# One order for all five engines, made by a planner inside the kernel: linear attention and two matrix products with sub-product tricks, on one core

## The chip, the core and the metric

The kernel runs on one core of a Trainium2 chip. Five engines take part: PE (matmul), DVE and POOL (elementwise work), ACT (elementwise work and functions) and SP, which here does nothing but start DMA transfers. Each engine runs its own instructions strictly in the order in which the program lists them; an instruction whose data or buffer is not ready holds everything behind it on that engine. The metric is the time of one execution on the device, in microseconds.

## The reference, cut to what matters

```
q, k, v: 8 batches x 8 heads x 576 x 64, float32;  the weights are float64
q_s = softmax(q, axis=-1);  k_s = softmax(k, axis=2)        # over d; over the sequence
kv  = einsum('bhsd,bhse->bhde', k_s, v)
x   = einsum('bhsd,bhde->bhse', q_s, kv)  -> 4608 tokens x 512
x   = max(x @ w_in, 0)**2 @ w_out                           # w_in 512 x 2048
out = (silu(x @ w_gate) * (x @ w_val)) @ w_out2             # w_gate, w_val 512 x 1536
```

## The kernel before

The 4608 tokens are cut into nine blocks of 512. Every product keeps float32 accuracy by splitting each operand into a rounded part and a rest ("hi" on ACT, `split`; "lo" by a subtraction, mostly on DVE) and multiplying three times (`mm3`, line 119). So PE's work is a long row of 128x512 matmuls, and each new operand costs an ACT and a DVE instruction before it.

There are four stretches. In the first, block 0 goes through attention and the first network; the order of all five engines is written out there as a list of step names (`FIRST_BLOCK`, line 381), and the change leaves this list alone. In the second, which I call the block stretch, blocks 1 to 4 go through the first network plainly: for each of 16 slices of the hidden layer 12 matmuls into a tile `ph`, then relu, square and split to a tile `g`, then 12 matmuls into `acc`. Beside it run the attention of the later blocks (`kv_unit`, `q_unit`: one for each block and pair of heads, results kept in DRAM as `x1d`) and the preparation of weights. In the third, the pair stretch, blocks 5 to 8 go through the first network as two pairs, with seven products in place of eight (`first_in`, `first_out`), in two halves each. In the fourth all blocks go through the second network the same way (`gated`, `out_stage`).

The seven products need sums of quarters of the weights, split into hi and lo. This preparation is one long generator, `work`: for the first network it loads float32 words that block 0 left in DRAM (`first_operands`); for the second it loads float64 weights (tile `wraw`), makes float32 words of them with one ACT and three DVE instructions (`bits_of`, tile `wbits`), forms four sums of quarters on POOL into new tiles `wsum` (lines 280 and 339), splits them into a staging tile `wst` (`stage`, line 252; there is one such tile until the last pair) and stores that in `hd`, `ad`, `gvd` or `od`. The stores are started from ACT's queue. A slice of a weight matrix pair is one set: 16 sets for the first network and 18 for the second. `Stream` later brings the operands back, 512 KB at a time, into five slots `wu`; a load waits until PE has left its slot.

What sets the order: SP's and PE's instructions run in the order of the program text (`manual_schedule`), where a counter (`Clock`, `attend`, `first_tick`) calls a step of attention or preparation at fixed places between matmul groups. The order of DVE, ACT and POOL is made by the framework's own scheduler.

Of the kernel before, what the change touches and what calls it, by code (L numbers as in the profile page):

```python
# [8 lines left out]
F32 = mybir.dt.float32  # L9
# [13 lines left out]
def tile_linear_attention_two_mlps(  # L23
# [12 lines left out]

# [45 lines left out]
    raws = st_prep.enter_context(tc.tile_pool(name="raws", bufs=2, side="right"))  # L96
    cv = st_prep.enter_context(tc.tile_pool(name="cv", bufs=5, side="right"))
# [39 lines left out]
    def bits_of(raws_):  # L137

        todo = []
        for raw in raws_:
            low, high = (
                raw.bitcast(I32).rearrange("p (n t) -> p n t", t=2)[:, :, t] for t in (0, 1)
            )
            w = cv.tile([P, T], I32, name="wbits", tag="wbits")
            todo.append((low, high, w, w))
        for low, high, w, t in todo:
            nc.scalar.activation(f32(t), f32(high), AF.Copy, scale=2.0**-112)  # L150
        for low, high, w, t in todo:
            nc.vector.tensor_scalar(
                t, t, 3, 0x7FFFFFFF, op0=ALU.logical_shift_left, op1=ALU.bitwise_and
            )
        for low, high, w, t in todo:
            nc.vector.scalar_tensor_tensor(
                t, low, 29, t, op0=ALU.logical_shift_right, op1=ALU.bitwise_or
            )
        for low, high, w, t in todo:
            nc.vector.scalar_tensor_tensor(  # L160
                w, high, -2**31, t, op0=ALU.bitwise_and, op1=ALU.bitwise_or
            )
        return [f32(w) for low, high, w, t in todo]

    class Weights:

        def __init__(self, src, order, borrow):
            self.src, self.order, self.borrow = src, order, borrow  # L170
            self.n_load = 0
            self.raw, self.done = {}, {}

        def load(self):
# [6 lines left out]
            if self.n_load <= 2 * self.borrow:  # L181
                t = w_slot(self.n_load - 1).rearrange("p t n -> p (t n)").bitcast(w.dtype)
            else:
                t = raws.tile([P, T], w.dtype, name="wraw", tag="wraw")
# [3 lines left out]
        def steps(self, n, pool):  # L188
# [18 lines left out]
            w = cv.tile([P, T], I32, name="wbits", tag="wbits")  # L207
# [15 lines left out]
    def w_slot(n):  # L223
# [7 lines left out]
        NF,  # L231
    )


    late = []

    def store(to, src, ticks=0):
        if ticks:
            late.append((clock.now + ticks, to, src))
        else:  # L240
            nc.sync.dma_start(to, src)

    def flush(until=None):
        for x in list(late):
            if until is None or x[0] <= until:
                nc.sync.dma_start(x[1], x[2])
                late.remove(x)

    stages = [(stp, "wst")]
    staged = [0]  # L250

    def stage():
        pool, tag = stages[staged[0] % len(stages)]
        staged[0] += 1
        return pool.tile([P, 2, 2, U], F32R, name="wst", tag=tag)

    made = set()

    def operands(kind, f):

        w, by_rows = {"gate": (w_gate, False), "val": (w_val, False), "out": (w_out2, True)}[kind]
        raw = []
        for s in (f, NG + f):
            t = raws.tile([P, T], w.dtype, name="wraw", tag="wraw")
            raw_load(w, by_rows, s, t)
            raw.append(t)
        yield
        first, = bits_of(raw[:1])
        yield
        second, = bits_of(raw[1:])  # L270
        yield
        a, b = first[:, 0:U], first[:, U:2 * U]
        c, d = second[:, 0:U], second[:, U:2 * U]

        def sums(n):
# [1101 lines left out]
```

## Time and profile before

| | |
|---|---|
| three runs | 1795.64, 1797.52 and 1800.48 us; median 1797.52 |
| the profiled execution | 1802.7 us, of which the span of its instructions is 1800.9 us |
| granted TensorE clock, mean over the span | 0.973 of full speed |
| block 1 to the last pair | from 123.5 to 1015.4 us, 891.9 us |

The two ends of the last row are the first matmul of block 1's attention product and the first matmul of the second network, read from the order of time on PE. The three terms of the kernel's time that matter below are PE's busy time in a stretch, its idle time there, and the clock that the chip granted; a clock of 1.00 is 2.4 GHz, and 0.50 would be the lower level of 1.2 GHz.

### The profile page before, as it was taken

How to read it: one execution, taken by the hardware profiler on the slowest of the kernel's cores; microseconds unless marked ns; L12 is line 12 of the kernel's file. 1: busy time of each engine (PE TensorE's matmuls, PEld its weight loads, DVE VectorE, ACT ScalarE, POOL GpSimd, SP SyncE). 2: the span in 40 equal slices, each digit the busy share in tenths (PEclk: the TensorE clock that was granted, in tenths of full speed). 3: DMA queues.
4: the chain of work that ended last, by engine and by line, in shares of the span. 5: the costliest groups of instructions: out<-in, count | busy, mean ns of one | idle time of the engine just before them, and what ended most of it. 6: DMA issues, size and time to landing. Idle time of an engine off the chain costs nothing.

```text
span 1800.9 us, 23969 instructions
## 1 busy us (share of the span) xinstructions
PE 1685.1 (94%) x8210; PEld 1366.9 (76%) x8210; DVE 1113.8 (62%) x1775; ACT 867.4 (48%) x1520; POOL 470.1 (26%) x428
## 2 busy tenths in 40 slices
PE   7999889989899898989898899999999999999998
PEld 5786667767677676867676678888888888888898
DVE  8874354565565476586868684854684568436656
ACT  7764344455455455454545453633463345334434
POOL 4753323331222422162313142101110220111011
PEclk9999999999999998999999899999999999999999
DMA  9958867655555496778788797786768667766897
GB/s 303 283 159 259 280 201 218 190 185 167 178 173 186 163 261 206 230 242 308 234 314 290 243 301 218 267 250 193 219 216 241 191 220 227 228 193 205 233 389 267
DMA packets 275017, 419.99 MB, mean 233 GB/s; under 512 B 126288, under 2 KB 167248, under 8 KB 274896
## 3 DMA queue, kind: packets, MB, share of 16 engines
q1 hardware_dynamic: 246992, 368.51, 65.9%
q10 hardware_dynamic: 27904, 49.95, 7.6%
q8 instruction: 66, 1.08, 0.2%
q14 instruction: 55, 0.45, 0.1%
HBM read 317.19 MB, written 101.19 MB: 232 GB/s over the span
## 4 chain that ended last, share of the span: by engine, by line
PE 57%; DMA 15%; DVE 9%; ACT 5%; POOL 4%; issue 3%; SPq 2%; ACTq 1%; DVEq 0%; POOLq 0%
PE ps L122 52%; DMA gvd<-wst 3%; DMA hd<-wst 3%; PE ph L122 2%; PE acc L122 2%; DVE wst L117 2%; DVE uo L117 2%; ACT wst L116 1%; DMA ad<-wst 1%; DMA wraw<-in_moe_w_val_dram 1%; DVE w L117 1%; DMA wraw<-in_moe_w_gate_dram 1%; DMA e<-x1d 1%; POOL wsum L280 1%; POOL wsum L339 1%
## 5 line engine op out<-in xcount | busy, mean ns | idle before, releaser
L122 PE MATMUL ps<-w,wu 128*128 128x512 f32 (+1 forms) x3192 | 682.6, 375 | 11.5 <-ACT ps L785 4.8
L122 PEld LDWEIGHTS ps<-w,wu 128*128 128x128 f32 x3192 | 567.7, 190 | 122.0 <-ACT ps L785 5.6
L122 PE MATMUL ps<-uo,wu 128*128 128x512 f32 (+1 forms) x1932 | 436.1, 386 | 24.0 <-DVE uo L117 21.7
L122 PEld LDWEIGHTS ps<-uo,wu 128*128 128x128 f32 x1932 | 351.5, 193 | 102.8 <-DVE uo L117 29.5
L122 PE MATMUL acc<-g,w 128*128 128x512 f32 x960 | 257.9, 416 | 22.0 <-ACT g L116 15.7
L117 DVE TENSOR_TENSOR uo<-u,uo 128x512 fp32r<-128x512 f32 (+1 forms) x322 | 229.8, 731 | 68.1 <-ACT uo L116 67.4
L116 ACT CAST uo<-u 128x512 fp32r<-128x512 f32 (+1 forms) x322 | 186.9, 592 | 159.4 <-PE ps L122 82.9
L122 PE MATMUL ph<-xT,w 128*128 128x512 f32 x960 | 247.7, 405 | 5.5 <-ACT xT L116 3.4
L122 PEld LDWEIGHTS acc<-g,w 128*128 128x128 f32 x960 | 185.7, 198 | 72.4 <-ACT g L116 18.9
L122 PEld LDWEIGHTS ph<-xT,w 128*128 128x128 f32 x960 | 180.0, 192 | 50.4 <-ACT xT L116 4.6
L953 POOL TENSOR_TENSOR u<-u 128x512 f32<-128x512 f32 (+1 forms) x30 | 35.4, 1180 | 619.2 <-DVE u L949 619.2
L948 DVE TENSOR_TENSOR u<-u,ps 128x512 f32<-128x512 f32 (+1 forms) x60 | 38.1, 634 | 195.1 <-ACT u L947 195.1
L900 ACT COPY ps<-ps 128x512 f32<-128x512 f32 x126 | 72.3, 574 | 136.1 <-PE ps L122 131.4
L117 DVE TENSOR_TENSOR wst<-wsum,wst 128x512 fp32r<-128x512 f32 x68 | 57.7, 848 | 117.3 <-ACT wst L116 117.3
L540 POOL TENSOR_TENSOR qs<-qs,qm 128x512 f32<-128x512 f32 x28 | 36.0, 1285 | 229.6 <-DVE qm L539 211.1
L116 ACT CAST wst<-wsum 128x512 fp32r<-128x512 f32 x68 | 48.2, 710 | 99.0 <-DMA gvd<-wst 27.3
L280 POOL TENSOR_TENSOR wsum<-wbits 128x256 f32<-128x256 f32 x36 | 35.2, 992 | 188.3 <-DVE wbits L160 112.8
L117 DVE TENSOR_TENSOR w<-x,w 128x512 fp32r<-128x512 f32 (+1 forms) x78 | 60.6, 785 | 23.6 <-ACT w L116 23.5
L117 DVE TENSOR_TENSOR g<-r,g 128x512 fp32r<-128x512 f32 x64 | 50.4, 788 | 39.0 <-ACT g L116 38.8
L605 ACT ACTIVATE r<-ph 128x512 f32<-128x512 f32 x64 | 38.2, 597 | 66.7 <-PE ph L122 41.1
L116 ACT CAST w<-x 128x512 fp32r<-128x512 f32 (+1 forms) x84 | 48.1, 585 | 43.6 <-PE ps L122 8.0
L339 POOL TENSOR_TENSOR wsum<-wsum 128x256 f32<-128x256 f32 x64 | 52.0, 812 | 52.0 <-DMA wsum<-w1d_out 21.3
(192 smaller groups left out, 1784.5 us busy)
## 6 DMA issues: line engine op xcount, KB each, us to landing
wu<-gvd SPq DMA_DIRECT2D x210, 512.0 KB, 4.4
wu<-od SPq DMA_DIRECT2D x105, 512.0 KB, 4.3
wu<-hd SPq DMA_DIRECT2D x56, 512.0 KB, 5.3
wu<-ad SPq DMA_DIRECT2D x56, 512.0 KB, 4.7
gvd<-wst ACTq DMA_DIRECT2D x84, 256.0 KB, 3.3
od<-wst ACTq DMA_DIRECT2D x42, 256.0 KB, 4.4
w<-in_moe_w_in_dram SPq DMA_DIRECT2D x16, 512.0 KB, 7.1
w<-in_moe_w_out_dram SPq DMA_DIRECT2D x16, 512.0 KB, 7.1
```

The lines of the kernel that those rows point to most:

```text
L116: nc.scalar.copy(hi, src)
L117: (eng or nc.vector).tensor_tensor(lo, src, f32(hi), op=ALU.subtract)
L122: nc.tensor.matmul(ps, lhsT=w[s], rhs=x[t], start=start and n == 0, stop=stop and n == 2, skip_group_check=more,)
L280: nc.gpsimd.tensor_tensor(to, x, y, op=op)
L339: nc.gpsimd.tensor_tensor(to, x, y, op=op)
L540: nc.gpsimd.tensor_tensor(t, t, m.unsqueeze(3).to_broadcast([P, TJ, 2, D]), op=ALU.add)
L605: nc.scalar.activation(r, ph, AF.Relu)
L900: nc.scalar.copy(x, y)
L948: nc.vector.tensor_tensor(u, u, gate, op=ALU.mult)
L953: nc.gpsimd.tensor_tensor(s1, a21, a22, op=ALU.add)
```

## The change

From block 1 to the end of the last pair all five engines now run in an order that a class `Plan` makes while the kernel is built. Each piece of work is a generator of steps. A step names its engine, a duration in microseconds, what it needs, which buffers it takes and frees, and, for a DMA, how long the data takes to land. `run` takes the step that can start first, and among those of its engine that could start within 0.3 us of it the one of the lowest rank (PE's chain through the blocks has helpers of rank 0, attention 2, weight preparation 5). Durations are constants in the code: 0.6 us for a 128x512 ACT instruction, 0.68 to 0.7 for one of DVE, 4.0 to 5.0 for a landing.

Along with it:

- `wst` has three buffers in place of one (two lent by the raw loads while the first network's sets are prepared), and its stores are started from SP, no longer from ACT, until the pairs are done.
- The four sums of quarters are made in place, on DVE, where POOL made them in new tiles.
- In `q_unit` POOL's subtraction of the maximum and ACT's exponential over 128x512 become eight ACT instructions of 128x64 that add the maximum as a bias and give the row sums; a DVE reduction goes.
- In the pairs the square after the relu moves from one DVE instruction to two of ACT, and the remaining POOL additions (`u`, `st`, `x`) move to DVE.
- More of the second network's sets are prepared later: counted in the two programs, raw loads in the block stretch, the pair stretch and after it go from 18, 14 and 4 to 9, 18 and 9. All later blocks' keys and values and most queries are handled in the block stretch (24 of `kv_unit` there, 20 before).

```diff
+    class Plan:
+        def after(self, engine, other):
+            if engine is None or engine == other:
+                return 0.0
+            return {"PE": 0.9, "SP": 1.0}.get(other, 0.2)
...
+        def run(self, until):
+            while not all(x in self.done for x in until):
+                todo = [(s, u) for u in self.units for s in (self.start(u),) if s is not None]
+                first, u = min(todo, key=lambda x: x[0])
+                engine = u[2][0]
+                s, u = min(
+                    (x for x in todo if x[1][2][0] == engine and x[0] <= first + 0.3),
+                    key=lambda x: x[1][0],
+                )
...
-    stages = [(stp, "wst")]
+    prep = {"stages": [(stp, "wst")] + [(raws, "raw0"), (raws, "raw1")], "raws": [], "n": 0, "r": 0}
+    prep.update(issue=nc.sync, plan=True, last={})
...
+        def put():
+            yield step("SP", 0.6 * k_, done, (), [keep], [key] if key else (), 4.0)
+            for j, to in enumerate(dests):
+                prep["issue"].dma_start(to, f32(t[0][:, j]))
...
-                nc.scalar.dma_start(to, f32(t[:, j]))
...
-            nc.gpsimd.tensor_tensor(to, x, y, op=op)
+            nc.vector.tensor_tensor(to, x, y, op=op)
...
+            yield step("SP", 0.8, (), [keep], (), [("ld", s, x)], 4.5)
+            t = raws.tile([P, T], w.dtype, name="wraw", tag=tag)
+            raw_load(w, by_rows, NG * x + f, t)
...
+        for x in range(TJ):
+            yield step("ACT", 0.6)
+            for h in range(2):
+                nc.scalar.activation(
+                    t[:, x, h], t[:, x, h], AF.Exp, bias=m[:, x, h:h + 1], accum_out=r[:, x, h:h + 1]
+                )
...
             if g == 0:
-                clock.tick()
-                next(work, None)
+                for _ in range(6):
+                    next(work, None)
```

First place: ACT in block 1, where the first network's weights are staged. `wst` is the staging tile, `r` and `g` are the chain behind PE's `ph`, `hd` the DRAM buffer. Before:

```order
L116 CAST wst_1723<-wsum_1669 128x2x256
L605 ACTIVATE r_1733<-ph_1704 128x512
L358 DMA hd0_153<-wst_1723 128x512 x2
L606 ACTIVATE r_1733<-r_1733 128x512
L116 CAST g_1736<-r_1733 128x512
L116 CAST wst_1728<-wsum_1670 128x2x256
L358 DMA hd0_153<-wst_1728 128x512 x2
```

And in the change, a little later in the same block (`qs` is a query tile, `qr` its row sums):

```order
L647 ACTIVATE qs_2000,qr_2065<-qs_2000,qm_2063 128x64 x4
L287 CAST wst_2123<-wsum_1984 128x2x256
L722 ACTIVATE r_2146<-ph_2125 128x512
L724 ACTIVATE r_2146<-r_2146 128x512
L287 CAST g_2149<-r_2146 128x512
L287 CAST wst_2152<-wsum_2040 128x2x256
```

The two stores of each staging tile have left ACT; the exponentials in small pieces have come in.

Second place: SP at the same point of the change, where those stores now stand (`wsum` loads feed the next set, `kt` and `vt` are keys and values, `e` holds a finished attention slice):

```order
L317 DMA hd1_154<-wst_2123 128x512 x2
L358 DMA wsum_2196<-w1d_in3_140 128x512
L317 DMA hd1_154<-wst_2152 128x512 x2
L669 DMA x1d2_130<-e_2202 128x512
L358 DMA wsum_2229<-w1d_in3_140 128x512
L476 DMA ad5_162<-w_1152 128x2x256
L511 DMA kt_2253<-in_k_dram 96x2x384
L518 DMA vt_182<-in_v_dram 96x6x64 x2
```

Loads of keys, values and weight words stand behind stores that wait for DVE.

Third place: the sums of one set in the pair stretch. Before, on POOL, between steps of the query units:

```order
L540 TENSOR_TENSOR qs_6026<-qs_6026,qm_6095 128x512
L549 TENSOR_TENSOR qs_6026<-qs_6026,qr_6191 128x512
L280 TENSOR_TENSOR wsum_6221<-wbits_6138 128x256
L280 TENSOR_TENSOR wsum_6221<-wbits_6031,wbits_6138 128x256
L280 TENSOR_TENSOR wsum_6222<-wbits_6138,wsum_6221 128x256
L280 TENSOR_TENSOR wsum_6222<-wbits_6031,wsum_6222 128x256
L117 TENSOR_TENSOR wst_6860<-wbits_6138,wst_6860 128x256
```

In the change, on DVE, between the evacuations of PSUM (`ps`) to the hidden tiles `u1`, their sums, and the operands `uo` that PE waits for:

```order
L1067 TENSOR_TENSOR u1_6429<-ps_6357,u1_6324 128x1024
L289 TENSOR_TENSOR wst_6418<-wbits_6364,wst_6418 128x256
L325 TENSOR_TENSOR wbits_6113<-wbits_6113,wbits_6364 128x256
L325 TENSOR_TENSOR wbits_6364<-wbits_6364 128x256
L1067 TENSOR_TENSOR u1_6324<-ps_6300,u1_6324 128x1024
L325 TENSOR_TENSOR wbits_6364<-wbits_6364,wbits_6113 128x256
L325 TENSOR_TENSOR wbits_6113<-wbits_6113,wbits_6364 128x256
L1081 TENSOR_TENSOR u1_6473<-u1_6324,u1_6429 128x1024
L1083 TENSOR_TENSOR u1_6324<-u1_6395,u1_6324 128x1024
L1085 TENSOR_TENSOR u1_6395<-u1_6429,u1_6324 128x1024
L1097 TENSOR_TENSOR uo_6492<-u1_6275,uo_6492 128x512
```

The preparation stands inside the chain of DVE work that feeds PE, and the words' own tiles are overwritten.

## Rows read from the trace of the kernel before

**Rows 1.** The page's first part: busy time, share, instructions of each engine.
```profile
PE 1685.1 (94%) x8210; PEld 1366.9 (76%) x8210; DVE 1113.8 (62%) x1775; ACT 867.4 (48%) x1520; POOL 470.1 (26%) x428
```

**Rows 2.** Busy time by stretch, in us, with instructions; the columns are the first line.
```profile
core 0: us, PE busy (x) PEld busy (x) DVE busy (x) ACT busy (x) POOL busy (x), PEclk, DMA share, GB/s
...
50.00:110.00 60.00, 56.89 (x310) 44.62 (x308) 55.17 (x98) 46.60 (x85) 47.62 (x43) 1.00 0.90 272
100.00:123.50 23.50, 23.06 (x122) 18.53 (x121) 16.59 (x31) 16.45 (x30) 16.86 (x15) 1.00 0.43 136
123.50:624.00 500.50, 449.23 (x2302) 350.33 (x2301) 261.40 (x482) 243.94 (x450) 154.62 (x164) 0.95 0.62 197
624.00:1015.40 391.40, 349.74 (x1518) 275.95 (x1519) 277.28 (x349) 193.89 (x285) 115.51 (x76) 0.94 0.79 256
1015.40:1080.00 64.60, 61.89 (x266) 49.14 (x265) 44.91 (x60) 33.00 (x51) 20.29 (x19) 1.00 0.92 305
```

**Rows 3.** PE in order of time, 105 to 125 us: start, duration (both us), what.
```profile
105.24 2.88 PE L122 MATMUL ph<-xT,w 128*128 128x512 f32 x12
107.96 0.84 PE L122 MATMUL acc<-g,w 128*128 128x512 f32 x3
...
117.81 0.92 PE L509 MATMUL pa<-wraw 96*64 96x65 f32 x24
...
123.54 1.11 PE L122 MATMUL ph<-qT,kv 128*128 128x64 f32 x6
124.49 0.60 PE L518 MATMUL pa<-ident,qs 128*128 128x128 f32 x4
```

**Rows 4.** Waits, 123.5 to 624 us: total, times, longest (us).
```profile
DVE wst L117 <- ACT wst L116: 103.3, 40, 6.1
...
ACT wst L116 <- DMA gvd<-wst: 28.1, 17, 3.3
...
ACT wst L116 <- DMA hd<-wst: 22.5, 12, 3.2
ACT wst L116 <- DMA ad<-wst: 19.6, 8, 4.5
...
PE acc L122 <- ACT g L116: 15.7, 11, 2.9
```

**Rows 5.** The longest wait of PE, 624 to 1015.4 us.
```profile
PE ps L122 <- DVE uo L117: 21.7, 14, 4.0
```

**Rows 6.** Groups by line and shape, DVE and POOL: busy us, mean ns; 624 to 1015.4 us.
```profile
L117 DVE TENSOR_TENSOR uo<-u,uo 128x512 fp32r<-128x512 f32 x112 | 96.4, 882 | 34.4 <-ACT uo L116 33.9
...
L809 DVE SCALAR_TENSOR_TENSOR u<-u 128x1024 f32<-128x1024 f32 x16 | 20.3, 1271 | 0.1
...
L833 DVE TENSOR_TENSOR u<-u,u 128x1024 f32<-128x1024 f32 x8 | 10.3, 1287 | 0.0
...
L852 POOL TENSOR_TENSOR u<-u,u 128x1024 f32<-128x1024 f32 x8 | 22.3, 2791 | 30.2 <-DVE uo L117 30.2
```

**Rows 7.** The same view of DVE, 1080 to 1750 us.
```profile
L117 DVE TENSOR_TENSOR uo<-u,uo 128x512 fp32r<-128x512 f32 x165 | 113.3, 704 | 28.0 <-ACT uo L116 27.9
```

**Rows 8.** Groups by shape, whole span or the first 123.5 us.
```profile
L977 DVE TENSOR_TENSOR u<-u 128x256 f32<-128x256 f32 x6 | 2.5, 424 | 0.2
...
L1120 ACT ACTIVATE w<-w,qm 128x64 f32<-128x64 f32 x16 | 5.3, 334 | 4.3 <-DVE qm L1106 4.3
```

**Rows 9.** Line 315, ACT's queue: instructions, duration in ns (min/median/max).
```profile
L315 ACTq DMA_DIRECT2D gvd<-wst x84: 325/327/1348, 367.7 to 867.3; - x84
```

**Rows 10.** DMA issues, 624 to 1015.4 us: count, KB each, median us to landing.
```profile
wu<-ad SPq DMA_DIRECT2D x56, 512.0 KB, 4.7
...
wraw<-in_moe_w_out_dram SPq DMA_DIRECT2D x8, 512.0 KB, 6.7
```

**Rows 11.** What SP's queue waited for: 618 to 1050 us, then 152 to 618.
```profile
SPq L675 <- PE ps L122: 249.2, 106, 8.4
...
SPq L246 <- DVE e L559: 18.9, 2, 13.9
```

More of the change, by code (lines that the diff above doesn't have):

```diff
@@ L252, in stage @@
[L252 to L255, printed above, removed]
-    made = set()
[L259 to L275, printed above, removed]
-            t = cv.tile([P, T], F32, name="wsum", tag="wbits")
-            return t, t[:, 0:U], t[:, U:2 * U]
+    word_no = [0, 0]
@@ L290, in operands @@
[L290 to L310 removed]
+            tt(d, d, b, ALU.subtract)
@@ L326, in first_to @@
+                for x, (source, names) in enumerate(todo):
+                    yield from out_of(source, names, keys[x], ("st", kind, f, x))
+            made.add((kind, f))
+    work = prepare()
     def first_to(kind, f, name):
@@ new lines, in in_part, with product @@
+    def in_part(k, p, half, m, ops):
+        xo = pair_x[p]
+        us = {}
+        def product(name, bank, start, needs=()):
+            for kind in range(2):
+                slot = stream.units // 2
+                need = [("wu", slot), *needs] + [("xo", xo.key, name, j) for j in range(NP // 2)]
+                take = [bank_take(k, bank)[1]] if start and not kind else ()
+                free, names = (), ()
+                if kind:
+                    free = [("slot", slot)]
+                    names = [("xdone", p, name)] if half and m else ()
+                yield step("PE", 1.361, need, take, free, names)
+                if start and not kind:
+                    open_bank(k, bank)
+                u = stream.next_unit()
@@ new lines, in out_part, with product @@
+                plan.unit(chunk(p, half, 4 * x + f, lambda us=us, w=where[name], j=j: us[w][:, j], needs, free), 1)
+        for m in range(2):
+            plan.unit(third(m), 0.9)
+        def product(name, bank, start, needs=()):
+            for f in range(NM // 2):
+                n = 4 * PRODUCTS.index(name) + f
+                slot = stream.units // 2
+                take = [bank_take(k, bank)[1]] if start and not f else ()
+                free = [("uo", (p, half, n))] + ([("slot", slot)] if f % 2 else [])
+                yield step("PE", 1.361, [("wu", slot), ("uo.", p, half, n), *needs], take, free)
+                if start and not f:
+                    open_bank(k, bank)
+                u = stream.next_unit()
+                x = chunks.pop((p, half, n))
```

1109 lines of the change are left out of this document (665 added, 444 removed).

## The prediction

> **What bounds the kernel now.** I began with the page's first part: PE is busy for 94% of the span [rows 1], and no other engine is above 62%. So only PE's idle time and its slow time can be won, and the question is where these lie. The table by stretch answers that [rows 2]. From 1015.4 us on PE is busy nearly throughout at a granted clock of 1.00. In the block stretch it is busy 449.2 of 500.5 us, in the pair stretch 349.7 of 391.4 us, and the clock there is 0.95 and 0.94. Idle time is thus 51.3 and 41.7 us, 93 us in all.
>
> A busy PE at half clock is not at its work's pace, so I counted the work. Twelve 128x512 matmuls take from 105.24 to 107.96 us, which is 0.2267 us each; the sums of keys and values of one `kv_unit` take 0.92 us; a query unit takes 0.95 us for its products (123.54 to 124.49) and up to 0.60 us for its transposes [rows 3]. The block stretch has 1536 matmuls and 12 left over from block 0, 350.9 us; 20 key and 20 query units, 49.4 us; and block 1's own four products with two transposes, 5.0 us. That is 405 us in 500.5, so 95 us are lost: 51 idle, 44 to the slower clock. The pair stretch has 1344 matmuls, 304.7 us, 4 key and 8 query units, 16.1 us: 321 us in 391.4, so 70 us are lost, 42 idle and 28 to the clock. These 165 us are the whole stake.
>
> Then the waits, to see what ends last. In the block stretch ACT waits for the stores of the one staging tile to land (28.1, 22.5 and 19.6 us), DVE then waits for ACT there (103.3 us), and PE waits longest for ACT's `g`, up to 2.9 us at a time [rows 4]. A store that is on its way holds ACT, and the chain behind PE's `ph` stands in the same queue. In the pair stretch PE waits for DVE's operands `uo`, 21.7 us [rows 5], and DVE is busy 277.3 of 391.4 us, ACT and POOL far less [rows 2]. So the bound in the first case is order and one buffer, in the second the load and order on DVE. No wait of the two stretches is one for arithmetic that PE lacks.
>
> **The change part by part.** *Three staging tiles and stores from SP.* The 70.2 us that ACT waited for landings [rows 4] should go almost wholly: three tiles let a store of some 4 us run under two more stagings. ACT loses the start of the stores as well, 0.327 us each [rows 9], 125 of them in the block stretch by the two orders, 41 us. The Trainium skill says of this move ("DMA: Bandwidth & Descriptors", section "Issuing engines are not separate DMA queues") that which engine starts a transfer changes only the time that its sequencer spends on it; by that rule the sum gains nothing but these starts, and the trace differs in that the landing held ACT, not the start.
>
> *Exponentials in pieces.* Eight instructions of 128x64, at 0.334 us [rows 8], are 2.7 us on ACT for a query unit; for 25 units 67 us are added, and the old 128x512 ones, about twice one of them by width, were part of ACT's 243.9 us [rows 2]. So ACT in the block stretch comes to roughly 244 - 41 + 67 + some 30 for four more key units and what goes with them, 300 us: the upper end. DVE loses the row sums and POOL the subtraction.
>
> *Sums of quarters on DVE.* One 128x256 operation takes 0.424 us [rows 8]. Some 80 move to the block stretch's DVE: 34 us, to 261 + 34, less what it sheds, about 280 us. In the pair stretch 36 move, 15 us; the eight additions of `u` that POOL made in 2.8 us each come to DVE at about 1.29 us, 10 us; x sums and half sums add some 12 us; 16 squares of 1.27 us leave for ACT, 20 us [rows 6]. Against this stands what POOL's presence costs DVE: the same `uo` subtraction takes 882 ns in the pair stretch and 704 ns after it [rows 6, 7]. With POOL nearly empty (3 instructions in the order) 112 of them give back 20 us. I count 277 + 15 + 10 + 12 - 20 - 20 - 10 for units moved away, 265 us; if DVE keeps the longer durations, 285 us. The Trainium skill has a rule against this direction ("Perfetto Trace Analysis", section "Optimizing Scalar/DVE Operations"): with DVE saturated, work may go to Scalar or even GpSimd; the same section warns that those two share a read port, so that offloading between them may not help. By the first half of the rule the pair stretch loses the 37 us that come to DVE; by the second they cost nothing, and the rows on `uo` speak for the second.
>
> *The order.* What can a fixed order of all five engines reach on this chip? The trace has a stretch of the same kind: block 0, whose order is a written list. Its last 23.5 us keep PE busy for 98.1% at clock 1.00, with ACT and DVE at about 70%; its thickest 60 us, where DVE is at 92% and the DMA share at 0.90, keep PE busy for 94.8% [rows 2]. These are my two bounds. The changed block stretch has 24 key and 25 query units: 350.9 + 60.8 + 5.0 = 417 us of PE work, 425 us at 98.1% and 440 at 94.8%. Its loads (ACT 300, DVE 280 of 425 us, 70% and 66%) are nearest to the former. The pair stretch has 304.7 + 4.7 = 309 us of PE work; DVE at 265 us is 81% of 326, and its DMA share rises (below), so it is nearest to the latter: 326 us.
>
> *Data that lands later than the planner counts.* It allows 5.3 us for a raw load (0.8 and 4.5), and these took 6.7 us in the pair stretch [rows 10]. ACT's first instruction on the words then holds ACT for about 1.5 us, 18 times in the pair stretch and 9 in the block stretch; PE has a group of 2.72 us and more of operands ahead, so I let half through: 14 and 7 us. Nothing and all of it (27 and 14) are the bounds. Loads of `wu`, 4.7 us [rows 10], are covered: five slots of 2.72 us, of which four are behind the one in use, leave 10.9 us from release to need.
>
> *DMA in the pair stretch.* It moved 256 GB/s at a share of 0.79 [rows 2], so 324 GB/s at a full share. Its 100 MB (256 GB/s times 391.4 us) become about 103 with four more raw loads and their stores, less the units moved ahead: 318 us at a full share. That lies just under 326 us; DMA is close to being the bound, which is why I do not take the better efficiency here.
>
> *After the pairs.* Nine raw loads remain in place of four, 2.5 sets, worked off six steps a product. A set is two raw loads and seven stores, 2.9 MB; 7.2 MB at the 305 GB/s of 1015.4 to 1080 us, where the DMA share is 0.92 already [rows 2], are 23 us; hidden or not, 0 to 23. I take 8, since PE there lost only 2.7 us with half as much to hide.
>
> **The sum.** Block 0's 123.5 us stay. Block stretch 425 + 7 = 432; pair stretch 326 + 14 = 340; after it 785.5 + 8 = 793.5. Together 1689 us of span. The old span was 1800.9 and its execution 1802.7 us; the median of three runs is 1797.5, 3.4 us under that span, so the same difference gives **1686 us**, 112 us less.
>
> **The rivals.** *Better still.* Late words cost nothing and the pair stretch also reaches 98.1%: 425 + 315, nothing lost after: 1649 of span, 1646 us. Against it is the DMA figure of 318 us; for it, that idle ACT and DVE time is 20 to 30%. *Data late throughout.* The planner treats every landing as a constant and DMA as without a limit. If the denser stretch moves bytes at the rate of 50 to 110 us, 272 GB/s [rows 2], the pair stretch takes 379 us; with the block stretch losing a third of what it lost (417 + 30) and all 23 us after: 1758 of span, 1755 us. *SP as the bound, the case on the other side.* SP's queue already stands for 249 us waiting for PE to free a slot, and once 13.9 us for a DVE copy before a store [rows 11]. Now each of 36 stagings in the pair stretch puts a store that waits for DVE ahead of the next `wu`. A slot has 10.9 us from release to need and the load takes 4.7, so 6.2 us of holding are free; what is beyond is PE's. To eat the 112 us each must hold SP for 6.2 + 3.1 = 9.3 us; at 10.5 us the loss is 155 and the time 1841 us. For it: an engine that falls behind a fixed order stays behind for all; against it: DVE has a fifth of its time free. *No gain*, because the lost time returns as other waits of the same length: 1797 us; the counts above give no mechanism, so a small chance.
>
> **How the numbers follow.** The forecast has 0.49 (1656 to 1715: the bounds of 425 to 440, of the late words and of the tail), better still 0.15, late throughout 0.22, SP 0.11, no gain 0.03. About 0.3% is what a measurement of this kernel can tell from no change. Faster by more than that: 0.49 + 0.15 + 0.22 = 0.86; within it 0.03; slower 0.11. The range that leaves out SP, no gain and a little at both ends is 1645 to 1760 us.
>
> **What the next profile would show.** Right: PE idle below 20 us in each of the two stretches and the clock at 0.98 or more; no wait of ACT for `hd`, `ad` or `gvd`; `uo` on DVE near 0.70 us; the pair stretch's DMA share near 0.95; the second network beginning near 895 us. Wrong: PE waits for `wu`, with SP held by a store (the SP rival); ACT waiting over 3 us for `wraw`, or `st` and `x` loads, in a row (late throughout); DVE busy over 95% of the pair stretch (my count of its load); PE idle over 10 us after the pairs (the tail).

## The result, and the profile after

The change takes 1726.43 us (median of four runs, 1726.18 to 1727.46) where the kernel before took 1799.0 us beside it. The ratio is 0.9595, with a 95% interval of 0.957 to 0.962: 72.6 us less. The forecast was 1686 us, with a range of 1645 to 1760.

The table by stretch of the kernel after follows [rows 2]: the stretch, its length, busy time of PE, of its weight loads, of DVE, ACT and POOL, then the granted clock, the DMA share and GB/s. The second stretch is the block stretch, the third the pair stretch; the last two are what comes after the pairs.

```profile
123.40:585.40 462.00, 434.35 (x2440) 345.01 (x2438) 265.52 (x560) 294.82 (x812) 28.53 (x25) 0.99 0.64 190
585.40:909.10 323.70, 319.09 (x1381) 256.56 (x1381) 239.25 (x351) 219.21 (x352) 4.27 (x4) 1.00 0.90 313
909.10:1010.00 100.90, 80.31 (x307) 61.97 (x305) 83.36 (x127) 51.77 (x78) 13.51 (x9) 0.90 0.82 299
1010.00:1725.70 715.70, 708.90 (x3474) 602.18 (x3474) 425.49 (x698) 302.34 (x539) 96.67 (x81) 1.00 0.75 235
```

Set against the forecast, the profiled execution (span 1725.7 us) divides as follows. The three errors have both signs, so part of them cancels in the sum.

| | before | forecast | after | off by |
|---|---|---|---|---|
| block stretch | 500.5 | 432 | 462.0 | +30.0 |
| pair stretch | 391.4 | 340 | 323.7 | -16.3 |
| after the pairs | 785.5 | 793.5 | 816.6 | +23.1 |

That is 36.8 us of span. The other 4 us of the 40 are a small term of the sum: the forecast took the median as 3.4 us under the span of the profiled execution, as it was in the kernel before; here it is 0.7 us over it.

The reader should see in the table that the pair stretch has only 323.7 - 319.1 = 4.6 us of idle PE time left, at full clock. The block stretch has 27.7 us, and the 101 us just behind the pairs have 20.6 us at a clock of 0.90. So the loss has moved, and the last piece of it is new.

What holds PE in the block stretch is read from its waits there [rows 4] (line waited for: us in total, times, longest):

```profile
PE pa L557 <- ACT kt L612: 10.2, 8, 1.8
PE pa L678 <- POOL qs L654: 8.4, 7, 1.9
PE pa L598 <- DVE m L595: 3.3, 6, 1.2
PE pa L604 <- DVE mx L601: 3.2, 5, 0.9
```

PE waits for `g`, 15.7 us of before, are gone, and of ACT's 70.2 us for `hd`, `ad` and `gvd` 0.4 us are left. In their place stand four waits, 25.1 us together, all for steps of attention: PE's fixed order has the transpose or product ahead of the moment at which its operand is done. What a wait costs beyond its own length shows in PE's order of time (start, duration):

```profile
412.87 2.96 PE L107 MATMUL acc<-g,w 128*128 128x512 f32 x12
417.50 0.92 PE L557 MATMUL pa<-vt,kt 96*64 96x65 f32 x24 [1.66 <-ACT kt L612]
418.35 4.61 PE L107 MATMUL ph<-xT,w 128*128 128x512 f32 x12
422.79 0.40 PE L107 MATMUL acc<-g,w 128*128 128x512 f32 x1
```

After 1.66 us of idleness the next twelve matmuls take 4.44 us from start to start, where twelve take 2.72 to 2.80 us elsewhere; the granted clock of 415 to 424 us is 0.81, so part of these 9 us ran at the lower level of 1.2 GHz. This short wait cost about twice its length. Not every such wait does: at 407.21 us PE had waited 1.32 us for `qs`, and the granted clock of 400 to 412 us stayed at 1.00.

Behind the pairs, these are the waits of PE and then of SP's queue, 909.1 to 1010 us:

```profile
PE ps L107 <- DMA wu<-gvd: 15.5, 5, 5.8
PE ps L107 <- ACT ps L1235: 2.6, 3, 1.0
```

```profile
SPq L115 <- DVE wbits L388: 48.2, 8, 16.5
```

Line 115 is the raw load. It stands at SP's head until DVE has read the tile that it overwrites, and loads of `wu` stand behind it. In SP's order of time, nothing starts between 938 and 950 us, and the next `wu` come right behind the raw load:

```profile
935.46 0.33 SPq L115 DMA_DIRECT2D wraw<-in_moe_w_out_dram  x1
935.89 1.42 SPq L829 DMA_DIRECT2D wu<-gvd  x2
950.12 0.33 SPq L115 DMA_DIRECT2D wraw<-in_moe_w_out_dram  x1
950.54 1.55 SPq L829 DMA_DIRECT2D wu<-gvd  x2
```

### The profile page after: what moved, and what is told of

It is laid out like the page before. It is cut to its first block, busy times and chain, and to the rows that moved or that the text cites. A ratio compares the mean times of both kernels' runs of the same rounds, so it can differ in the third digit from the quotient of the medians.

```text
span 1725.7 us, 24332 instructions
## 1 busy us (share of the span) xinstructions
PE 1651.0 (96%) x8210; PEld 1348.8 (78%) x8210; DVE 1116.6 (65%) x1923; ACT 961.1 (56%) x1972; POOL 223.2 (13%) x206
## 4 chain that ended last, share of the span: by engine, by line
PE 75%; ACT 6%; DMA 5%; DVE 5%; issue 2%; POOL 1%; SPq 0%; ACTq 0%; DVEq 0%; POOLq 0%
PE ps L107 56%; PE ph L107 9%; PE acc L107 6%; PE pa L557 1%; ACT qs L647 1%; PE pa L107 1%; DMA wu<-gvd 1%; DMA gvd<-wst 1%; ACT r L724 1%; DMA od<-wst 1%; ACT r L722 1%; ACT g L287 1%; DMA vt<-in_v_dram 1%; PE pa L678 1%; ACT wst L287 0%
## 5 line engine op out<-in xcount | busy, mean ns | idle before, releaser
L107 PE MATMUL ps<-w,wu 128*128 128x512 f32 (+1 forms) x3192 | 687.9, 377 | 26.2 <-DMA wu<-gvd 15.5
L107 PE MATMUL ps<-uo,wu 128*128 128x512 f32 (+1 forms) x1932 | 418.3, 378 | 0.3 <-DVE uo L1097 0.3
L101 ACT CAST uo<-u 128x512 fp32r<-128x512 f32 (+1 forms) x210 | 119.9, 579 | 111.6 <-PE ps L107 42.4
L102 DVE TENSOR_TENSOR uo<-u,uo 128x512 fp32r<-128x512 f32 (+1 forms) x210 | 133.0, 651 | 31.8 <-ACT uo L101 31.6
L654 POOL TENSOR_TENSOR qs<-qs,qr 128x512 f32<-128x512 f32 x28 | 32.0, 1142 | 462.6 <-DMA gvd<-wst 80.4
L1097 DVE TENSOR_TENSOR uo<-u,uo 128x512 fp32r<-128x512 f32 x112 | 73.3, 686 | 23.6 <-ACT uo L1095 23.4
L1095 ACT CAST uo<-u 128x512 fp32r<-128x512 f32 x112 | 66.4, 620 | 23.8 <-PE ps L107 22.7
L647 ACT ACTIVATE qs<-qs,qm 128x64 f32<-128x64 f32 x224 | 75.1, 337 | 7.7 <-DVE qm L642 5.2
L287 ACT CAST wst<-wbits 128x512 fp32r<-128x512 f32 (+1 forms) x72 | 51.0, 715 | 36.8 <-DVE wbits L388 22.4
L289 DVE TENSOR_TENSOR wst<-wbits,wst 128x512 fp32r<-128x512 f32 (+1 forms) x72 | 56.4, 789 | 22.2 <-ACT wst L287 20.6
L1282 ACT ACTIVATE u<-ps 128x512 f32<-128x512 f32 (+1 forms) x60 | 33.3, 555 | 49.7 <-PE ps L107 48.1
```

The lines of the kernel that those rows point to most:

```text
L101: nc.scalar.copy(hi, src)
L102: (eng or nc.vector).tensor_tensor(lo, src, f32(hi), op=ALU.subtract)
L107: nc.tensor.matmul(ps, lhsT=w[s], rhs=x[t], start=start and n == 0, stop=stop and n == 2, skip_group_check=more,)
L287: nc.scalar.copy(hi, src)
L289: nc.vector.tensor_tensor(lo, src, f32(hi), op=ALU.subtract)
L647: nc.scalar.activation(t[:, x, h], t[:, x, h], AF.Exp, bias=m[:, x, h:h + 1], accum_out=r[:, x, h:h + 1])
```

## The experiments

Twelve kernels ran. My theory after the result had three parts: (a) the block stretch loses because the planner puts attention steps of PE a microsecond too early; (b) the time after the pairs is longer because leftover raw loads hold SP; (c) the pair stretch gained more than forecast because POOL's absence shortens DVE. The rivals are named with each run. All stretches and waits are read from each run's profiled execution; the median of its runs can differ from that by a few us. Times to compare are 1726.43 us for the change, and 1799.5 to 1801.7 us for the kernel before beside these runs.

**Half the pace behind the pairs (tail3).**

```diff
-                for _ in range(6):
+                for _ in range(3):
```

> The changed kernel with three preparation steps for each product after the pairs, in place of six. My theory: the 31 us too many after the pairs (816.6 us against 785.5 before) come from raw loads at the head of SP's queue that wait for DVE to have read the raw tile, with loads of wu behind them. With half the pace DVE has read the tile by then: the hold of SP by wbits (48.2 us, longest 16.5) falls under 15 us, PE's waits for wu after 909 us fall from 15.5 to under 5 us, and the time falls by 10 to 20 us, to 1706 to 1716. Rival 1, DMA as the limit of that stretch (299 GB/s there): the same bytes still have to move, PE's waits move further back, and the time stays within 5 us of 1726. Rival 2, too slow a pace: the last sets come late, PE waits for them in the second network's later groups, and the time is over 1735.

Measured: 1714.43 us (ratio to before 0.953, 0.949 to 0.957). PE's wait for `wu` falls from 15.5 to 5.2 us, and SP's hold by `wbits` is gone from the stretch:

```profile
PE ps L107 <- DMA wu<-gvd: 5.2, 2, 3.8
PE ps L107 <- ACT ps L1235: 2.9, 3, 1.7
```

The 12.0 us are within the theory's range; DMA as the limit is refuted, for the stretch moves the same 297 GB/s with 11 us less idleness of PE.

**Raw loads from another queue (rawpool).** Pace of six, but no `wu` behind a raw load:

```diff
-    def raw_load(w, by_rows, f, t):
+    def raw_load(w, by_rows, f, t, eng=None):
...
-            raw_load(w, by_rows, NG * x + f, t)
+            raw_load(w, by_rows, NG * x + f, t, None if prep["plan"] else nc.gpsimd)
```

> The changed kernel, six steps a product after the pairs as in the change, but the raw loads there are started from POOL's queue, so that loads of wu never stand behind one. My theory, SP's head held by them: PE's waits for wu (15.5 us between 909 and 1010 us) fall under 5 us and the time by 8 to 18 us, to 1708 to 1718. Rival 1, DVE's load there (83%) is the loss and the queue only shows it: PE waits for ps, s and p in place of wu, and the time stays within 5 us of 1726. Rival 2: POOL, held by a raw load that waits for DVE, is late with its own sums, and the time is 1730 or more.

Measured: 1721.5 us, 4.9 us less, just inside the first rival's 5 us. PE's waits change their names more than their sum, from 15.5 + 2.6 to 5.3 + 13.4 us:

```profile
PE ps L107 <- ACT ps L1235: 13.4, 6, 3.5
PE ps L107 <- DMA wu<-gvd: 5.3, 1, 5.3
```

So part (b) was too narrow. SP's head is where the loss showed. The better lever is the pace: with half of it (tail3) the two waits add up to 8.1 us, with another queue to 18.7 as against 18.1. That six preparation steps a product put more on ACT and DVE ahead of what PE needs next than fits beside one product is the reading that fits both runs; no run shows it by itself.

**A margin for attention on PE (margin1).** In the planner, a step of an attention unit on PE whose forerunner ran on another engine starts 1.0 us later than the durations say:

```diff
+            if engine == "PE" and 2 < u[0] < 3 and u[4] not in (None, "PE"):
+                s = max(s, u[3] + self.after(u[4], engine) + 1.0)
```

> The changed kernel whose planner lets an attention step of PE that follows a step of another engine start 1.0 us later than its durations say. My theory: the 27.7 us of PE's idle time in the block stretch are attention steps that stand in PE's fixed order ahead of their operand (kt, qs, m, mx), because the planner's durations are a little short. With the margin PE's waits for these four fall from 24 us to under 8, the block stretch from 462 to 440 to 450 us, and the time to 1706 to 1716. Rival 1: the planner's lateness accumulates from other engines (ACT or DVE behind plan), so that a constant margin moves the same waits to other steps: PE idle stays over 20 us and the time within 5 us of 1726. Rival 2: attention finished later makes later steps late, and the time rises over 1732.

Measured: 1698.59 us (0.944, 0.940 to 0.947), 27.8 us less. The block stretch, and PE's waits in it for the same operands (lines have moved by two):

```profile
123.40:564.70 441.30, 428.90 (x2434) 344.76 (x2433) 273.68 (x570) 296.49 (x808) 28.18 (x24) 0.99 0.67 204
```

```profile
PE pa L559 <- ACT kt L614: 3.0, 3, 1.8
...
PE pa L606 <- DVE mx L603: 0.8, 1, 0.8
```

The stretch is 20.7 us shorter and the idle time 12.4 in place of 27.7 us; the four waits for attention come to 4.1 in place of 25.1 us. The time fell below the range expected, because another 8 us are gained behind the pairs (808.6 us), which the theory did not foresee: 9 raw words are left there in place of 11, but PE still waits 15.5 us for `wu`, so what brought these 8 us stays open. Part (a) holds for the block stretch.

**Two durations put right (durtrue).** On top of tail3, without a margin:

```diff
-            yield step("ACT", 0.6)
+            yield step("ACT", 0.67)
...
-        yield step("POOL", 1.1)
+        yield step("POOL", 1.16)
```

> Three steps a product after the pairs, no margin, and the two durations of the query unit that the planner has clearly too short set to what the trace shows: a pair of exponentials starts 0.667 us after the pair before it (the plan has 0.6, four to a unit) and POOL's product takes 1.154 us (the plan has 1.1). Question: is the margin's gain of 28.7 us (1714.4 to 1685.8) these two figures, 0.34 us a unit on the way to qs, or slack in general? My theory: general, since PE waited 1.2 us at a time, and for kt, m and mx too, whose steps are costed nearly right: PE's waits for qs (8.4 us) fall to 4 to 7, the others stay, and the time is 1703 to 1713. Rival, that these two figures are the cause: 1695 or less.

Measured: 1709.62 us, 4.8 us under tail3, the block stretch 457.9 us; the waits of PE:

```profile
PE pa L557 <- ACT kt L612: 6.5, 5, 1.8
PE pa L678 <- POOL qs L654: 6.4, 8, 1.5
PE pa L604 <- DVE mx L601: 4.1, 8, 0.8
PE pa L598 <- DVE m L595: 3.5, 7, 0.8
```

The time and `qs` are in the range expected, but the wait for `kt` fell as well (from 10.2 us), which the theory had staying. The two figures explain some 5 of the margin's 29 us. What helps is slack in general, not better constants for these two; whether a full set of true durations would do as much was not tried.

**Both repairs (combo).** Margin of 1.0 us and three steps a product.

> Both repairs together: the planner's margin of 1.0 us for attention steps on PE, and three preparation steps a product after the pairs. My theory: the two losses lie in different stretches and the preparation left for the end is the same, so the gains add: 27.8 us and 12.0 us under the change's 1726.4 are 1686.6, and I expect 1682 to 1692. Rival: the earlier start of the second network takes over part of the tail's loss (DMA, or DVE late there), so that the sum is 1693 to 1699.

Measured: 1685.75 us (0.936, 0.934 to 0.938), against a sum of 1686.6. Block stretch, pair stretch and the rest:

```profile
123.40:564.06 440.66, 429.74 (x2440) 345.46 (x2438) 273.14 (x570) 296.51 (x808) 29.02 (x25) 0.99 0.67 205
564.06:887.45 323.39, 318.19 (x1383) 256.33 (x1382) 243.24 (x355) 222.59 (x361) 4.23 (x4) 1.00 0.90 315
887.45:1684.50 797.05, 781.90 (x3781) 659.23 (x3779) 505.59 (x810) 348.42 (x610) 111.30 (x90) 1.00 0.75 245
```

This version beats both kernels; the losses were independent, as expected.

**A larger margin (combo15).** 1.5 us in place of 1.0.

> Both repairs with the margin at 1.5 us in place of 1.0. With 1.0 us PE's waits for attention's operands in the block stretch are already down to some 4 us, and its idle time to 11 us. My theory: there is hardly anything left for a margin, so the time is within 4 us of 1685.75. Rival: the waits that are left (kt 1.8 us at a time) need more than 1.0 us, and the time falls to 1681 or less; or attention becomes late as a whole, 1690 or more.

Measured: 1684.9 us, no difference from combo that these runs can tell. The block stretch is 437.4 us, of which 9.4 idle.

**One staging tile (onestage).** The change with the two further tiles taken away:

```diff
-    prep = {"stages": [(stp, "wst")] + [(raws, "raw0"), (raws, "raw1")], "raws": [], "n": 0, "r": 0}
+    prep = {"stages": [(stp, "wst")], "raws": [], "n": 0, "r": 0}
...
-                prep["stages"].remove((raws, "raw0"))
...
-                prep["stages"].remove((raws, "raw1"))
```

> The changed kernel with one staging tile throughout, as before, and all else of the change, the planner included, which knows that there is only one. A staging then takes about 0.7 + 0.7 us for its two halves, 0.6 to 2.4 us on SP and 4 us to land, some 6.5 to 8 us, and the next cannot begin: 62 in the block stretch are 400 us or more of 462, 36 in the pair stretch 250 to 290 of 324. My theory: the planner puts other work on ACT and DVE while the tile is in flight, so PE is hardly held, but preparation runs behind and more of it is left for the time after the pairs: 1735 to 1775. Rival 1, the order is all: within 5 us of 1726. Rival 2, the three tiles are the gain: 1785 or more.

Measured: 1754.48 us, 28 us more, as the theory had it. The block stretch is 6 us longer, the pair stretch 2 shorter; the rest is 24 us longer:

```profile
123.40:591.50 468.10, 436.56 (x2449) 345.63 (x2448) 244.87 (x519) 286.36 (x801) 29.45 (x26) 0.99 0.57 168
591.50:912.90 321.40, 316.83 (x1373) 255.07 (x1371) 235.26 (x346) 216.25 (x341) 3.14 (x3) 1.00 0.91 313
912.90:1753.20 840.30, 793.77 (x3781) 665.92 (x3779) 536.00 (x871) 363.36 (x637) 110.69 (x90) 0.97 0.76 248
```

With one tile the planner gets less prepared (DVE 244.9 in place of 265.5 us in the block stretch, DMA 168 in place of 190 GB/s), and 18 raw words are left for the end.

**Three tiles in the old order (before3).** The kernel before, with the tiles alone:

```diff
-    stages = [(stp, "wst")]
+    stages = [(stp, "wst"), (raws, "wraw"), (raws, "wraw")]
...
+        del stages[1:]
```

The second line takes the two further tiles away as soon as the first network's sets are prepared. The changed kernel has two tiles from there on, and three again once attention is done.

> The kernel before, with three staging tiles while the first network's sets are prepared, its order otherwise as it was and its stores still on ACT. My theory: ACT's waits for hd and ad (42 us) go, PE's waits for g shorten from 15.7 us to about half, but the waits that come from the order of steps stay: a gain of 5 to 25 us, 1774 to 1794. Rival 1, the order is all: within 5 us of 1799. Rival 2, the three tiles make most of the gain: 1760 or less.

Measured: 1793.08 us, ratio 0.9954 (0.993 to 0.998): some 8 us. ACT's waits in the block stretch show why it is no more [rows 4]:

```profile
ACT r L606 <- PE ph L122: 62.0, 30, 7.1
ACT wst L116 <- POOL wsum L339: 38.1, 20, 5.3
ACT wst L116 <- DMA gvd<-wst: 31.3, 17, 4.1
```

The 42.1 us for `hd` and `ad` are gone, but the wait for POOL's sums, 16.4 us in this stretch of before, is 38.1 us now, and that for `gvd`, whose sets have one tile in this kernel as before, is about as long as it was. Three tiles for the first network's sets alone are worth a ninth of the gain; what more tiles for the second network's sets would do in the old order was not tried. The rest of the change without the tiles gives 1754 us. In that rest the planner and the moves from engine to engine stand together: no run has the old order with the moves, and the exponentials in pieces and the squares on ACT were never taken back by themselves.

**Stores from ACT again (actstores, comboact).** First the change with one edit, then the same edit in combo:

```diff
-    prep.update(issue=nc.sync, plan=True, last={})
+    prep.update(issue=nc.scalar, plan=True, last={})
...
-            yield step("SP", 0.6 * k_, done, (), [keep], [key] if key else (), 4.0)
+            yield step("ACT", 0.35 * k_, done, (), [keep], [key] if key else (), 4.0)
```

> The changed kernel with the staging stores started from ACT again, in the planned order and with three tiles. ACT gets about 0.33 us for each of some 125 starts in the block stretch (41 us on 295 of 462) and 72 in the pair stretch (24 us on 219 of 324). My theory: ACT has room for it and nothing waits for landings, so PE loses a little by later chains: 1726 to 1742. Rival 1, that moving the stores to SP was a main part of the gain: 1750 or more. Rival 2, that stores on SP waiting for DVE hold loads that PE needs: 1722 or less.

Measured: 1720.57 us, 5.9 us less than the change. No expectation named 1720.6 for the right reason: the second rival has the number, but PE waits for `wu` as long as before behind the pairs (16.6 us), so loads held behind stores weren't the loss there. The block stretch is 6.5 us shorter, the pair stretch 6.6 longer, and the rest 7.3 shorter.

> Both repairs, and the staging stores started from ACT as before the change. With the change alone that brought 6 us: the block stretch 6.5 us shorter, the pair stretch 6.5 longer, the time after the pairs 7 shorter. My theory: the shorter block stretch came of attention steps that happened to be later in PE's order, which the margin gives already, and the tail's part of a smaller rest, so that what is left is the pair stretch's loss: 1684 to 1694. Rival: SP's queue itself is the cost (stores there held it for 59 us waiting for DVE), and the time is 1681 or less.

Measured: 1690.05 us, 4.3 us more than combo: in the theory's range, but not for its reason. Block and pair stretch are 5.3 and 2.5 us shorter than combo's, the rest is 12.6 longer; there 12 raw words are left, and with three steps a product the last sets come too late for PE (waits after 980 us):

```profile
PE ps L107 <- DMA wu<-od: 6.0, 2, 3.6
PE ps L107 <- DVE uo L102: 3.5, 2, 2.9
```

The engine that starts the stores is worth nothing sure, one way or the other. How much is left for the end does not explain the sign: actstores has 12 raw words left against the change's 11 and a shorter rest.

**The sums of quarters on POOL (poolsums).**

```diff
-            nc.vector.tensor_tensor(to, x, y, op=op)
+            nc.gpsimd.tensor_tensor(to, x, y, op=op)
...
-        yield step("DVE", 0.8)
+        yield step("POOL", 1.8)
```

(The last edit stands twice, once for each pair of sums.)

> The changed kernel with its four sums of quarters back on POOL (in place, as in the change, and planned there), in every stretch. DVE is relieved of some 36 us in the block stretch and 30 us in the pair stretch. My theory: POOL's presence makes DVE's other instructions longer, uo in the pair stretch from 686 to 740 to 850 ns, so DVE gains little or nothing, and the steps that wait for DVE come later than planned: 1728 to 1755. Rival, that DVE's load is what counts: uo stays under 720 ns, DVE falls to 210 us or less in the pair stretch, and the time is 1724 or less.

Measured: 1731.68 us (0.9617, 0.9585 to 0.9648), 5 us more than the change, with intervals that overlap. The time is in the theory's range, its reason is not: `uo` is 698 ns, hardly longer than after the change (686). DVE falls to 226.6 us in the pair stretch, not to the rival's 210. The mean hides what a meeting costs: 109 of the 112 `uo` took 0.69 us; three began while a quarter sum ran on POOL and took 0.91 to 1.23 us. Few met, and so the mean hardly moved.

**The long sums of `u` on POOL (poolu).** In the pair stretch, 24 sums of 128x1024:

```diff
-            yield step("DVE", 1.22, [("u", k, "22"), ("u", k, "12")], [key("s1")], (), [("op", k, "5")])
+            yield step("POOL", 2.8, [("u", k, "22"), ("u", k, "12")], [key("s1")], (), [("op", k, "5")])
...
-            nc.vector.tensor_tensor(s1, a21, a22, op=ALU.add)
+            nc.gpsimd.tensor_tensor(s1, a21, a22, op=ALU.add)
...
```

(The other two sums are moved in the same way.)

> The changed kernel with the three sums of u of each product group (24 instructions of 128x1024 in the pair stretch) on POOL in place of DVE, planned there with 2.8 us each. In the trace of before a uo subtraction on DVE that met such a POOL sum took 2.06 us and its neighbours 0.69 us; the quarter sums of 128x256 on POOL, in the run ahead of this one, lengthened uo only to 698 ns. My theory: it is the long POOL sums that hold DVE's instructions, so uo's mean goes back from 686 to between 780 and 900 ns, and of the 29 us that leave DVE in the pair stretch at least half return as longer instructions; PE waits for u and uo and the time is 1732 to 1760. Rival, that uo was long in before for another reason (its order, its operands' banks): uo stays under 720 ns, DVE's busy time falls by 25 us or more, and the time is within 6 us of 1726.

Measured: 1741.87 us, 15.4 us more, in the range expected. DVE's costliest groups in the pair stretch (times, busy us, mean ns) and the stretch itself:

```profile
L1095 DVE TENSOR_TENSOR uo<-u,uo 128x512 fp32r<-128x512 f32 x112 | 82.2, 763 | 29.3 <-ACT uo L1093 29.1
L289 DVE TENSOR_TENSOR w<-x,w 128x512 fp32r<-128x512 f32 x24 | 22.2, 923 | 9.8 <-ACT w L287 9.8
L289 DVE TENSOR_TENSOR wst<-wbits,wst 128x512 fp32r<-128x512 f32 x26 | 21.3, 821 | 15.9 <-ACT wst L287 13.8 <-DMA x<-x2d 2.1
```

```profile
585.32:930.28 344.96, 324.40 (x1382) 258.91 (x1381) 243.25 (x333) 220.76 (x355) 65.33 (x28) 0.99 0.84 297
```

PE's largest wait in this stretch, 0.3 us in the change:

```profile
PE ps L107 <- DVE uo L1095: 13.1, 8, 3.3
```

The pair stretch is 21.3 us longer than in the change, and the time after it 7.4 shorter. `uo` came out a little under the range I gave (763 ns, 780 forecast as the least), but DVE's busy time rose from 239.3 to 243.3 us although it had 18 instructions fewer: what was taken off it came back as longer instructions. How, shows in single instructions. Here POOL's sum and the `uo` that met it:

```profile
634.73 2.93 POOL L1083 TENSOR_TENSOR u<-u,u 128x1024 f32<-128x1024 f32 x1
```

```profile
635.32 2.89 DVE L1095 TENSOR_TENSOR uo<-u,uo 128x512 fp32r<-128x512 f32 x1
```

And in the trace of before:

```profile
698.16 2.85 POOL L852 TENSOR_TENSOR u<-u,u 128x1024 f32<-128x1024 f32 x1
```

```profile
699.50 2.06 DVE L117 TENSOR_TENSOR uo<-u,uo 128x512 fp32r<-128x512 f32 x1
```

POOL ends at 637.66 and 701.01 us, `uo` at 638.21 and 701.56: each `uo` stood until POOL was through, and ended 0.55 us behind it. The other long ones are alike. In the pair stretch of poolu four of 112 `uo` began while a sum ran on POOL; they took 2.83 to 2.89 us, the others 0.68 to 0.69, and all four ended 0.55 us behind the sum, as did the three of poolsums behind their short ones. In before 21 of 112 took over 0.75 us, and each of them began while POOL ran; in the change none did. So short sums hold DVE too, for as long as they run, and the share of `uo` that meets POOL sets the mean.

The Trainium skill ("SBUF — State Buffer", section "SBUF: two separate sides") says that the two engines share a pair of ports as a lock which the first holds for its whole instruction, and that a DVE instruction with two operands from SBUF, or in a mode that uses both ports, is blocked by it. The trace agrees: four `u<-ps` of before, with one operand from PSUM, began while POOL ran and still took 1.21 to 1.22 us, their usual time, and in poolu a TENSOR_SCALAR with one operand from SBUF took 2.65 us beside a sum, where it takes 0.42 alone (which mode it ran in the trace does not show).

**What decides the time after the pairs.** All kernels together (raw words left for that part, counted by ACT's conversions; one profiled execution each):

| kernel | words left | steps a product | us after the pairs |
|---|---|---|---|
| before | 4 | | 785.5 |
| before3 | 4 | | 790.2 |
| combo | 9 | 3 | 797.1 |
| combo15 | 10 | 3 | 797.9 |
| tail3 | 11 | 3 | 800.4 |
| durtrue | 11 | 3 | 801.2 |
| comboact | 12 | 3 | 809.6 |
| margin1 | 9 | 6 | 808.6 |
| poolu | 10 | 6 | 809.2 |
| rawpool | 11 | 6 | 808.8 |
| the change | 11 | 6 | 816.6 |
| actstores | 12 | 6 | 809.3 |
| poolsums | 13 | 6 | 816.3 |
| onestage | 18 | 6 | 840.3 |

The kernel before and before3 have the same program in this part and lie 4.7 us apart, so differences of that size say little. Half the pace is worth 12 to 16 us with the same number of words (margin1 and combo, the change and tail3). The number of words shows at its ends, 4 and 18, and at three steps with 12 words (comboact), where the last sets came too late; between 9 and 13 words at six steps the times are 809 or 816 us without an order. What separates these two groups stays open.

## Why the prediction came out as it did

The direction was right, and so were the waits that the forecast wanted gone: ACT's for landings, PE's for `g`, and DVE's long `uo`. How much of the gain is the planner's order and how much the moves between engines is not shown, since no run parts them; the two further tiles are worth 28 us in the new order. That 1726 us is not further from 1686 owes something to luck, for +30.0 and +23.1 us were met by -16.3; without the last it would be 1743, still in the stated range. It lies outside the forecast's own case, 1656 to 1715; the upper ends of the bounds named there add up to 1736, so that 1715 was too low for its own terms. Of the signs listed, the clock (0.99 and 1.00), ACT's waits for landings (0.4 us) and `uo` (686 ns) came as forecast (the landings in the block stretch; in the pair stretch 1.0 us); idle time was under 20 us in only one of the two stretches, the DMA share of the pair stretch was 0.90 in place of 0.95, and the second network began at 909 in place of 895 us. Of the signs against, the last one came: PE idle by over 10 us after the pairs.

**The block stretch: 425 us was too small.** The step that failed is "its loads are nearest to the former", that is to block 0's 98.1%. I had looked at the loads of the engines and not at how PE's fixed order meets theirs. ACT and DVE came out at 294.8 and 265.5 us, even under my 300 and 280; yet PE stood for 27.7 us, 25.1 of them for operands of attention, a price that the 23.5 us of block 0 behind the 98.1% do not have (0.4 us idle). The margin showed it: 441 us, the upper of my two bounds (440). The other part of the error is in the 417 us of PE work itself: combo's PE is busy for 429.7 us at a clock of 0.99. So up to 13 of the 44 us that I put down to the slower clock in the block stretch of before may not have been lost to it, but have been work that I had counted too short. I took 2.72 us for twelve matmuls from block 0 [rows 3]; in the block stretch of the kernel after, groups start 2.72 us apart in some places and 2.80 in others:

```profile
146.16 2.96 PE L107 MATMUL acc<-g,w 128*128 128x512 f32 x12
148.96 2.96 PE L107 MATMUL ph<-xT,w 128*128 128x512 f32 x12
151.76 0.63 PE L107 MATMUL acc<-g,w 128*128 128x512 f32 x2
...
437.09 2.88 PE L107 MATMUL acc<-g,w 128*128 128x512 f32 x12
439.81 2.88 PE L107 MATMUL ph<-xT,w 128*128 128x512 f32 x12
442.53 1.53 PE L107 MATMUL acc<-g,w 128*128 128x512 f32 x6
```

At 2.80 throughout, 128 groups would be 10 us. What sets this pace stays open. The 7 us for late words were not needed: ACT had no wait for `wraw` among its twelve largest there.

**The pair stretch: 340 us was too much.** Of 326 + 14, the 14 for late words measured nearly nothing (ACT waited 8.2 us for words, and PE's idle time of the whole stretch is 4.6 us), and the 94.8% was too cautious: PE is busy for 98.6%. Two counts were wrong on the safe side. DVE came to 239 us, not 265. And 324 GB/s at a full DMA share, taken from before, was too low a ceiling: after the change 313 GB/s take a share of 0.90, which by the same rule is 348. So DMA was not close to being the bound, and the rival of data late throughout had no ground in this stretch. The doubt that I weighed against the rule of the Trainium skill ("Perfetto Trace Analysis", section "Optimizing Scalar/DVE Operations") on moving work to POOL came out on the side of the row on `uo`, and poolu shows it by itself. The two engines that share a read port by that section are DVE and POOL, not ACT.

**After the pairs: 8 us was too small, and its upper bound of 23 too.** The loss is 31 us: PE is idle for 27.4 us there, 7.3 before, and busy 11 us longer, with the clock at 0.90 in the first 101 us. The count was short as well: 11 raw words were left, not nine. I priced the further sets by the bytes that they move, and left out the pace; three steps a product in place of six take back 12 us (tail3; 16 us of this part in the two profiled executions). What the 15 us consist of by which that run's part is still longer than before is not shown.

**The rivals.** SP as the bound did not come: SP was held 33.9 us by stores waiting for `wst` in the pair stretch, 3.9 us at most at a time, and PE waited for no `wu` there. All holds were shorter than the 6.2 us that I had counted as free. The better case, 1646 us, was nearest in the pair stretch (323.7 against the 315 that it took); as a whole no kernel here reached it. *Data late throughout* took 379 us for the pair stretch at 272 GB/s; it moved 313 GB/s. That combo lands on 1685.75 us, next to my 1686, does not make the forecast right: its block stretch is 9 us longer, its pair stretch 17 shorter than I had them.

## What to carry to other kernels

A planner with constant durations puts one engine's steps in front of operands that come a microsecond late; on the engine that bounds the kernel, give side work a margin before tuning any constant, since an early side step holds the main chain, and one that came 1.0 us later cost nothing that shows here. Count the work that a new order leaves for the end, and try the pace at which it is worked off: its bytes alone gave too small a price here. And before moving elementwise work to POOL, or when judging what work there costs, look in the trace at the DVE instructions that begin while POOL runs, one by one: a mean over all of them hides the price of a meeting.

## What was unexpected of the hardware

- The small exponentials with a row sum carry a second instruction each. On ACT in the block stretch:

```profile
L647 ACT ACTIVATE qs<-qs,qm 128x64 f32<-128x64 f32 x196 | 65.7, 336 | 7.7 <-DVE qm L642 5.2 <-issue 1.5 <-DMA vt<-in_v_dram 1.0
L647 ACT ACTIVATION_READ_ACCUMULATOR qs<-qs,qm 128x1 f32 x196 | 36.7, 187 | 0.0
```

The two overlap, and one pair follows the next after 0.333 us, so the price stays near my 0.334 us; the planner's 0.6 us for two is a tenth short.
- A wait of PE of 1.66 us was followed by twelve matmuls that took 4.44 us in place of 2.8, with a granted clock of 0.81 over the 9 us around them.
- Twelve matmuls of one shape have two paces, 2.72 and 2.80 us, inside one stretch.
